# Batch 2's Q and K transposed by PE from 1 KB loads in an attention and MoE kernel, and x^T of batch 3 by DMA

## Chip, cores, metric

One core of one Trainium2 chip. The metric is device time in microseconds (us) of one execution. PE is TensorE (PEld its weight loads), DVE VectorE, ACT ScalarE, POOL GpSimd, and SP the queue that issues most DMAs. All of PE's matmuls in the profile write to the tiles o, acc, h and st; the program puts these in PSUM and calls them banks. All comparisons use fast runs (granted TensorE clock 0.99 to 1.00). A ratio is the mean time of one kernel's fast runs over that of the other's in the same rounds on the same chip, so it isn't quite the ratio of the medians quoted beside it.

## The reference, cut to what matters

```python
# q, k, v: (8 batches, 8 heads, 576 positions, 64)
scores = q @ k.T / 8;  keep 0 <= i - j < 64;  softmax;  attn @ v      # sliding window
x = attn_out.transpose(0, 2, 1, 3).reshape(4608, 512)
h = x @ w_in                                   # 512 x 2048
out = (h * clip(h + 3, 0, 6) / 6) @ w_out      # 2048 x 512
```

## The kernel before

The token axis is cut into nine tiles of 512. Tile T runs stage 1 (16 groups of 4 matmuls with w_in; ACT and DVE make the gate of each group) and stage 2 (64 matmuls with w_out). Attention of a later batch is threaded between the groups: `SS` (scores, exponent on ACT, mask product on DVE), `N_` (P times V and the normalization on DVE), and x^T either by PE (`X_`, 5 transposes and a copy on ACT) or by DMA (`xt_dma`). Heads go in pairs g = 0 to 3.

Q and K have to be transposed too. Batches 0 and 1 are loaded in 1 KB rows and transposed by PE, batches 2 to 7 are loaded in 256-byte rows, cast on POOL and transposed by DMA.

```python
def load_for_dma(b):                 # 256-byte rows, five loads each of q, k, v, on the SP queue
    ...
def transpose_pairs_by_dma(self):    # batch 2: eight DMA transposes
    for g in range(NG):
        for n, T in ((qn_all, self.QT), (kn_all, self.KT)):
            nc.sync.dma_start_transpose(out=T[:, g, :]..., in_=n[:, g, :, :, :]...)

def main_t(self, g, i, tr, copy=None):       # batches 0, 1: four PE transposes into PSUM tile tr
    ...
    def evac(): (copy or (vcopy, acopy)[i])(out=(self.QT, self.KT)[i]..., in_=tr...)  # Q by DVE, K by ACT
def rest_t(self, tr):                        # the last 64 positions of q and k, one PSUM tile
    ...
    def evac():
        vcopy(out=self.QT[:, :, SM:S], in_=tv[:, :, 0, :])
        (acopy if self.b else vcopy)(out=self.KT[:, :, SM:S], in_=tv[:, :, 1, :])

def s1_bank(fc, T):                          # PSUM of stage 1, group fc, here for T == 1
    if fc in (12, 13): ...                   # o, acc
    if fc % 4 < 2: return h_bank()[:]        # h0, h1
    return ...                               # st0, st1

def pieces(bt):                              # what follows group i of stage 1, piece i of stage 2
    if bt.b == 2:                            # in tile 1
        return p1, {1: [f(SS, 0)], 2: [f(SS, 1)], 4: [f(N_, 0), f(SS, 2)], 6: [f(X_, 0)], ...}
    if bt.b == 3:                            # in tile 2
        return {13: [f(SS, 0)]}, {0: [f(SS, 1)], 3: [f(N_, 0), f(SS, 2)], 5: [f(X_, 0)], ...}
    p1 = {10: [f(SS, 0)], 13: [f(SS, 1)]}    # batches 4 to 7: x^T by DMA
    p2 = {0: [f(SS, 2)], 1: [f(N_, 0)], 2: [f(SS, 3)], 3: [f(N_, 1), f(xt_dma, 0)], ...}
```

The softmax here doesn't subtract the row's maximum and nothing guards it: scores larger than these inputs give would overflow.

Of the kernel before, what the change touches and what calls it, by code (L numbers as in the profile page):

```python
# [24 lines left out]
def kernel(  # L25
# [9 lines left out]
    nc = tc.nc  # L35
    P = nc.NUM_PARTITIONS
# [3 lines left out]
    NG = H // 2  # L40
# [57 lines left out]
        return out  # L98

    class LoadsForPE:  # L100
        def __init__(self, b):
            self.b = b
            self.qst = stage.tile([P, H, R * D], F32, name="qst", tag="qst")
            self.kst = stage.tile([P, H, R * D], F32, name="kst", tag="kst")
            self.rst = stage.tile([P, H, D], F32, name="rst", tag="rst")
            self.tiles = (self.qst, self.kst, self.rst)

        def main(self, i, h0, h1):
            nc.gpsimd.dma_start(
                out=self.tiles[i][:, h0:h1, :],  # L110
                in_=(q, k)[i][self.b, h0:h1, 0:SM, :].rearrange("h (p j) d -> p h (j d)", j=R),
            )

        def rest(self):
            for i, src in enumerate((q, k)):
                nc.gpsimd.dma_start(
                    out=self.rst[i * SR : (i + 1) * SR, :, :],
                    in_=src[self.b, :, SM:S, :].rearrange("h s d -> s h d"),
                )

    def load_v_by_head(b):
        vst = stage.tile([P, KB, H, D], F32, name="vst", tag="vst")
        ins = load_blocks(vst, v, b, (KB - 1,), SR) + load_v(b, vst, 0, H)
        return vst, ins

    def load_for_dma(b):
        sts, ins = [], []
        for n, src in (("qst", q), ("kst", k), ("vst", v)):
            t = stage.tile([P, KB, H, D], F32, name=n, tag=n)
            ins += load_blocks(t, src, b, range(KB), SR if src is v else 0)  # L130
            sts.append(t)
        return tuple(sts), ins
# [34 lines left out]
    def keep_busy(n):  # L167
# [11 lines left out]
        out=mask1[:], in_=mask1[:], pattern=[[1, QW]], compare_op=ISGE,  # L179
# [3 lines left out]
        out=mask1[:], in_=mask1[:], pattern=[[-1, QW]], compare_op=ISGE,  # L183
        fill=0.0, base=WINDOW - 1, channel_multiplier=1,
    )
    qn_all = consts.tile([P, NG, KB, 2, D], BF16, name="qn")
    kn_all = consts.tile([P, NG, KB, 2, D], BF16, name="kn")
# [3 lines left out]
    for o0, m0, m1 in ((0, 0, QW), (QW, 0, QW), (2 * QW, 0, QW), (3 * QW, 0, P), (3 * QW + P, WINDOW, P)):  # L191
        nc.vector.tensor_scalar(
            out=maskneg[:, o0 : o0 + m1 - m0], in0=mask1[:, m0:m1],
# [45 lines left out]
    vcopy, pcopy, acopy = nc.vector.tensor_copy, nc.gpsimd.tensor_copy, nc.scalar.copy  # L239

    class Batch:
# [28 lines left out]
        def transpose_by_dma(self):  # L270
            for n, T in ((qn_all, self.QT), (kn_all, self.KT)):
# [1 line left out]
                    out=T[:].rearrange("d g (k s) -> d (g k) s", s=P),  # L273
                    in_=n[:].rearrange("p g k h d -> p (g k h d)"),
                )

        def transpose_pairs_by_dma(self):
            for g in range(NG):
                for n, T in ((qn_all, self.QT), (kn_all, self.KT)):
                    nc.sync.dma_start_transpose(  # L280
                        out=T[:, g, :].rearrange("d (k s) -> d k s", s=P),
                        in_=n[:, g, :, :, :].rearrange("p k h d -> p (k h d)"),
                    )

        def cast_qk(self, st, i, h0, heads, copy):
            n = (qn_all, kn_all)[i][:].rearrange("p g k h d -> p (g k h d)")[:, 0 : R * H * D]
# [237 lines left out]
    def s1(T, first=()):  # L524
        t0 = T * TB
        gT = gpool.tile([P, NFC, TB], BF16, name="gT")
        gTs[T] = gT

        def mms(fc, hT, gs):
            for g in gs:  # L530
                nc.tensor.matmul(  # L531
                    hT, lhsT=win16[:, g, fc * P : (fc + 1) * P],
                    rhs=xT[:, g, t0 : t0 + TB], start=(g == 0), stop=(g == NG - 1),
                )

        def gate(out, hT, shape):
            t1 = (t1pool, t2pool)[len(shape) - 2].tile(shape, BF16, name=f"t{len(shape) - 1}")
            nc.scalar.activation(out=t1[:], in_=hT, func=RELU, bias=half[:], scale=1.0 / 6.0)  # L538
            nc.vector.scalar_tensor_tensor(  # L539
                out=out, in0=t1[:], scalar=1.0, in1=hT, op0=MIN, op1=MULT,  # L540
            )

        if first:
            sts = [ps_st.tile([P, 2, 512], F32, name=f"st{u}") for u in range(2)]
            for gs in first:
                for fc in range(4):
                    mms(fc, sts[fc // 2][:, fc % 2, :], gs)
                yield
            for u in range(2):
                for fc in (2 * u, 2 * u + 1):  # L550
                    mms(fc, sts[u][:, fc % 2, :], (NG - 1,))
                gate(gT[:, 2 * u : 2 * u + 2, :], sts[u][:], [P, 2, TB])
                yield
                yield
        for fc in range(4 if first else 0, NFC):
            hT = s1_bank(fc, T)
            mms(fc, hT, range(NG))
            gate(gT[:, fc, :], hT, [P, TB])
            yield
# [25 lines left out]
    def run(gen, n=10 ** 6):  # L585
        for _ in range(n):
            if next(gen, "end") == "end":
                break
# [4 lines left out]
    def o_acc_tr():  # L593
        while True:
            yield ps_o.tile([P, 1024], BF16, name="o")
            yield ps_acc.tile([P, 1024], BF16, name="acc")

    oa_tr = o_acc_tr()
# [14 lines left out]
    def N_(bt, g, banks=None):  # L613
        n = [pv(bt, g, h, next(banks) if banks else h_bank()) for h in range(2)]
        n[0]()
        n[1]()

    def X_(bt, g, st=None):
        xt_pe(bt, g, h_tr() if st is None else ps_st.tile([P, 2, 1024], BF16, name=f"st{st}")[:, 0, :])()
# [17 lines left out]
    def cast_pairs(bt, st, h0, heads):  # L637
        bt.cast_qk(st, 0, h0, heads, pcopy)
        bt.cast_qk(st, 1, h0, heads, pcopy)


    bt, st = Batch(0), stage0
# [9 lines left out]
    ld = LoadsForPE(1)  # L652
# [9 lines left out]
    def T0_(g):  # L662
# [40 lines left out]
    m = s1(0, ((0, 1), (2,)))  # L703
# [12 lines left out]
        out=mask[:], in_=mask1[:].unsqueeze(1).to_broadcast([P, 2 * (KB - 1), QW])  # L716
    )
    for h in range(2):
        nc.vector.tensor_copy(
            out=mask[:, (KB - 1) * (h + 1) - 1, P:QW], in_=mask1[:, WINDOW : 2 * WINDOW],  # L720
        )
    bt, st = Batch(1), st1
# [18 lines left out]
    bt.cast_v_end(vst1, pcopy)  # L741
    for g in range(NG):
        bt.cast_v(vst1, 2 * g, 2 * g + 2, pcopy)
    st2, _ = load_for_dma(2)

    def st_tr(u):
        t = ps_st.tile([P, 2, 1024], BF16, name=f"st{u}")
# [2 lines left out]
    def st_pair(u):  # L750
        t = ps_st.tile([P, 2, 512], F32, name=f"st{u}")
        return iter((t[:, 0, :], t[:, 1, :]))
# [6 lines left out]
    m = s2(0, BY_PART)  # L759
# [33 lines left out]
    rest_x(bt0, 1)  # L793
    go()
    X_(bt, 0)
    N_(bt, 2, st_pair(0))
    X_(bt, 1, 1)
    N_(bt, 3, oa)
    X_(bt, 2)

    def stage_(T, bt, pieces1, pieces2):
        if T < 3:
            m = s1(T, ((0, 1), (2,)))
            run(m, 1)
            X_(Batch(T), NG - 1)
            run(m, 1)
        else:
            m = s1(T)
        for i in range(NFC):
            run(m, 1)  # L810
            for f in pieces1.get(i, ()):
                f()
        m = s2(T, BY_BLOCK)
        for i in range(16):
            run(m, 1)
            for f in pieces2.get(i, ()):
                f()

    def pieces(bt):
        if bt is None:  # L820
            return {}, {}
        f = lambda fn, *a: lambda: fn(bt, *a)
        p1, p2 = {}, {}
        if bt.b == 2:
            return p1, {
                1: [f(SS, 0)], 2: [f(SS, 1)], 4: [f(N_, 0), f(SS, 2)], 6: [f(X_, 0)], 7: [f(N_, 1), f(SS, 3)],
                9: [f(X_, 1)], 10: [f(N_, 2)], 12: [f(X_, 2)], 13: [f(N_, 3)],
            }
        if bt.b == 3:
            return {13: [f(SS, 0)]}, {  # L830
                0: [f(SS, 1)], 3: [f(N_, 0), f(SS, 2)], 5: [f(X_, 0)], 6: [f(N_, 1), f(SS, 3)],
                8: [f(X_, 1)], 9: [f(N_, 2)], 11: [f(X_, 2)], 12: [f(N_, 3)], 14: [f(X_, 3)],
            }
        p1 = {10: [f(SS, 0)], 13: [f(SS, 1)]}
        p2 = {
            0: [f(SS, 2)], 1: [f(N_, 0)], 2: [f(SS, 3)], 3: [f(N_, 1), f(xt_dma, 0)],
            5: [f(xt_dma, 1)], 6: [f(N_, 2)], 8: [f(N_, 3), f(xt_dma, 2)], 10: [f(xt_dma, 3)],
        }
        return p1, p2

    bt2 = Batch(2)
    bt2.cast_for_dma(st2, (0, 1))
    for u0, osb in held:
        nc.gpsimd.dma_start(out=out[u0 : u0 + P, :], in_=osb[:])
    bt2.cast_for_dma(st2, (2,))
    bt2.transpose_pairs_by_dma()
    nxt, pend = bt2, None
    for T in range(1, NTB):
        p1, p2 = pieces(nxt)
        b = T + 2  # L850
        nxt = None
        if b < B:
            sts, _ = load_for_dma(b)
            nxt = Batch(b)
            p1.setdefault(12 if T == 1 else 6, []).append(
                lambda bt=nxt, sts=sts: bt.cast_for_dma(sts)
            )
            p2.setdefault(6 if T < 3 else 12, []).append(lambda bt=nxt: bt.transpose_by_dma())
        stage_(T, None, p1, p2)


# [28 lines left out]
```

## Time and profile before

| | us |
|---|---|
| time, median of 4 fast runs | 313.4 (312.6 to 314.3) |
| profile that the prediction had | span 351.8, clock 0.85 (slow state) |
| profile taken later | span 314.8, clock 1.00 |

The first profile fell in the slow state. An experiment on another chip gave one at full clock. The stretches of it below are stage 1 and stage 2 of tile 1, then of tile 2. The columns are: stretch, its length, busy time and count of PE, PEld, DVE, ACT, POOL, clock, DMA share, GB/s.

```profile
58.94:73.78 14.84, 14.43 (x72) 6.52 (x70) 9.83 (x15) 10.71 (x15) 10.21 (x16) 1.00 1.04 211
73.78:94.06 20.28, 19.01 (x184) 10.45 (x183) 10.33 (x22) 10.32 (x16) 3.54 (x7) 1.00 0.96 187
94.06:109.74 15.68, 14.89 (x80) 6.80 (x79) 9.12 (x13) 11.68 (x17) 5.96 (x8) 1.00 1.03 227
109.74:128.25 18.51, 18.51 (x179) 10.42 (x178) 10.20 (x22) 9.53 (x15) 6.40 (x10) 1.00 1.13 211
```

A stage of pure matmuls (tiles 7 and 8) takes 13.81 us, 215.8 ns a matmul (12 of them take 2.59 us in the changed kernel's full-clock profile too, from 125.15 to 127.74). What is above that is attention's PE work or a wait.

### The profile page before, as it was taken

To read this page: it belongs to the slowest core of one execution; us is meant where nothing else is said; L and a number is where in the kernel's file an instruction comes from. 1 tells how busy PE (TensorE), PEld (TensorE's weight loads), DVE (VectorE), ACT (ScalarE), POOL (GpSimd) and SP (SyncE) were. 2 spreads that over 40 slices of the span, in tenths; PEclk is the share of its full clock that TensorE was granted. 3 is DMA by queue.
4 is the path that set the end of the run, shared out by engine and by line. 5 is a ranking of instruction groups with operands and counts; after the bars stand their busy time and mean duration, and the time that the engine had idled before them with its cause. 6 is when DMAs were issued, how large, how long until landed. Compare 5 with 4: busy or idle time off the path is not lost.

```text
span 351.8 us, 5579 instructions
## 1 busy us (share of the span) xinstructions
PE 339.5 (97%) x2125; PEld 158.6 (45%) x2162; DVE 177.9 (51%) x334; ACT 178.3 (51%) x264; POOL 94.1 (27%) x137
## 2 busy tenths in 40 slices
PE   7989998999999999999999999999999999999995
PEld 3534445444544554445444544454445444444442
DVE  4648546575418662776177616772477336106600
ACT  3757545566437644682268316831585146216511
POOL 6856355630540640334006500460000000000000
PEclk9888888888888888888888888888888888888888
DMA  7999999989999993992799669966600710010011
GB/s 250 174 255 234 210 170 215 211 208 185 195 212 251 208 231 110 218 181 69 193 221 213 122 162 235 197 136 128 168 3 30 113 53 0 31 61 30 0 61 60
DMA packets 147579, 52.80 MB, mean 150 GB/s; under 512 B 136384, under 2 KB 142528, under 8 KB 147552
## 3 DMA queue, kind: packets, MB, share of 16 engines
q1 hardware_dynamic: 141920, 44.18, 61.6%
q0 software_dynamic: 5360, 8.00, 11.4%
q8 instruction: 17, 0.28, 0.4%
q10 hardware_dynamic: 272, 0.26, 0.2%
q14 instruction: 10, 0.08, 0.1%
HBM read 36.70 MB, written 9.44 MB: 131 GB/s over the span
## 4 chain that ended last, share of the span: by engine, by line
PE 89%; DMA 4%; issue 2%; DVE 1%; ACT 1%; SPq 0%; POOL 0%; POOLq 0%
PE h L531 19%; PE o L568 19%; PE acc L568 18%; PE st L531 9%; PE o L531 7%; PE acc L531 7%; PE st L354 4%; DMA win<-in_moe_w_in_dram 2%; PE h L384 2%; PE h L568 2%; DMA qst<-in_q_dram 1%; PE h L389 1%; PE h L417 1%; ACT pT L362 1%; DMA vst<-in_v_dram 1%
## 5 line engine op out<-in xcount | busy, mean ns | idle before, releaser
L531 PEld LDWEIGHTS <-win 128*128 128x128 bf16 x576 | 59.6, 105 | 81.1 <-DMA win<-in_moe_w_in_dram 1.3
L568 PEld LDWEIGHTS <-gT 128*128 128x128 bf16 x576 | 56.3, 105 | 68.3 <-issue 0.5
L568 PE MATMUL o<-wout,gT 128*128 128x512 bf16 x261 | 73.0, 421 | 1.0 <-issue 0.3
L568 PE MATMUL acc<-wout,gT 128*128 128x512 bf16 x261 | 71.6, 421 | 0.8
L531 PE MATMUL h<-xT,win 128*128 128x512 bf16 x259 | 71.9, 421 | 0.4
L362 ACT ACTIVATE pT<-st 128x768 bf16<-128x768 f32 x64 | 48.8, 808 | 18.4 <-PE st L354 18.3
L539 DVE SCALAR_TENSOR_TENSOR gT<-t,st 128x512 bf16<-128x512 bf16 (+1 forms) x26 | 20.8, 809 | 69.5 <-ACT t L538 69.5
L538 ACT ACTIVATE t<-h,half 128x512 bf16<-128x512 f32 x66 | 44.7, 690 | 15.2 <-PE h L531 15.2
L539 DVE SCALAR_TENSOR_TENSOR gT<-t,h 128x512 bf16<-128x512 bf16 x66 | 44.6, 684 | 14.4 <-ACT t L538 14.4
L372 DVE TENSOR_TENSOR pT<-pT,mask 128x1536 bf16<-128x1536 bf16 x28 | 31.2, 1116 | 26.8 <-ACT pT L362 26.8
L258 POOL CAST qn<-qst 128x512 bf16<-128x512 f32 x24 | 14.8, 654 | 86.7 <-DMA qst<-in_q_dram 86.7
L531 PE MATMUL st<-xT,win 128*128 128x512 bf16 x124 | 34.3, 423 | 1.5 <-DMA win<-in_moe_w_in_dram 1.3
L574 ACT COPY osb<-acc 128x512 f32<-128x512 f32 x17 | 10.0, 586 | 49.8 <-PE acc L568 49.8
L574 ACT COPY osb<-o 128x512 f32<-128x512 f32 x17 | 10.0, 587 | 36.3 <-PE o L568 36.3
L531 PE MATMUL o<-xT,win 128*128 128x512 bf16 x91 | 26.9, 422 | 0.2
L531 PE MATMUL acc<-xT,win 128*128 128x512 bf16 x90 | 26.9, 422 | 0.2
L538 ACT ACTIVATE t<-st,half 128x512 bf16<-128x512 f32 (+1 forms) x26 | 20.1, 785 | 9.7 <-PE st L531 9.7
L406 DVE TENSOR_TENSOR opg<-h,rec 128x320 bf16<-128x320 f32 x48 | 23.6, 491 | 1.7
L384 PEld LDWEIGHTS <-pT 128*128 128x128 bf16 x256 | 18.6, 100 | 9.5 <-DVE opg L406 1.3
L248 POOL CAST V<-vst 128x512 bf16<-128x512 f32 (+1 forms) x14 | 17.3, 1233 | 18.5 <-DMA vst<-in_v_dram 15.9
L538 ACT ACTIVATE t<-acc,half 128x512 bf16<-128x512 f32 x23 | 15.8, 687 | 7.0 <-PE acc L531 7.0
L258 POOL CAST kn<-kst 128x512 bf16<-128x512 f32 x24 | 14.6, 648 | 17.4 <-DMA kst<-in_k_dram 14.4
(107 smaller groups left out, 293.4 us busy)
## 6 DMA issues: line engine op xcount, KB each, us to landing
out_dram<-osb SPq DMA_DIRECT2D x32, 256.0 KB, 2.3
qst<-in_q_dram SPq DMA_DIRECT2D x28, 256.0 KB, 4.6
kst<-in_k_dram SPq DMA_DIRECT2D x27, 256.0 KB, 5.3
vst<-in_v_dram SPq DMA_DIRECT2D x24, 256.0 KB, 5.4
vst<-in_v_dram SPq DMA_DIRECT2D x23, 128.0 KB, 4.6
win<-in_moe_w_in_dram POOLq DMA_DIRECT2D x4, 512.0 KB, 8.8
wout<-in_moe_w_out_dram POOLq DMA_DIRECT2D x4, 512.0 KB, 13.8
qst<-in_q_dram POOLq DMA_DIRECT2D x2, 512.0 KB, 12.3
```

The lines of the kernel that those rows point to most:

```text
L248: copy(out=self.V[:, 0 : KB - 1, h0:h1, 0:D], in_=vst[:, 0 : KB - 1, h0:h1, :])
L258: pcopy(out=n[:, g, 0 : KB - 1, :, :].rearrange("p k h d -> p k (h d)"), in_=s[:, 0 : KB - 1, 2 * g : 2 * g + 2, :].rearrange("p k h d -> ...
L354: nc.tensor.matmul(st[:, h, o0 : o0 + n], lhsT=bt.KT[h * D : (h + 1) * D, g, k0 : k0 + P], rhs=bt.QT[h * D : (h + 1) * D, g, q0 : q0 + n], ...
L362: nc.scalar.activation(out=pT[:, :, 2 * u : 2 * u + 2, 0:QW], in_=st[:, :, 0:w].rearrange("p h (k w) -> p h k w", k=2), func=EXP, scale=scale,
L372: nc.vector.tensor_tensor(out=pT[:, :, :, 0:QW], in0=pT[:, :, :, 0:QW], in1=mask[:].rearrange("p (h k) w -> p h k w", h=2), op=MULT,)
L384: nc.tensor.matmul(ob, lhsT=pT[:, h, qb, 0:P], rhs=V[:, qb, 2 * g + h, :], start=True, stop=(qb == 0),)
L406: nc.vector.tensor_tensor(out=opgs[bt.b, g][:, 0:nb, h, :], in0=ov[:, :, 0:D], in1=rec[:, 0:nb].unsqueeze(2).to_broadcast([P, nb, D]), op= ...
L531: nc.tensor.matmul(hT, lhsT=win16[:, g, fc * P : (fc + 1) * P], rhs=xT[:, g, t0 : t0 + TB], start=(g == 0), stop=(g == NG - 1),)
L538: nc.scalar.activation(out=t1[:], in_=hT, func=RELU, bias=half[:], scale=1.0 / 6.0)
L539: nc.vector.scalar_tensor_tensor(out=out, in0=t1[:], scalar=1.0, in1=hT, op0=MIN, op1=MULT,)
L568: nc.tensor.matmul(accs[ts], lhsT=gT[:, fc, ts * P : (ts + 1) * P], rhs=wout16[:, fc, :], start=(fc == 0), stop=(fc == NFC - 1),)
L574: acopy(out=osb[:], in_=accs[ts])
```

## The change

The intent is to relieve the DMA queues in the first third of the kernel, where they are full (a DMA share of 0.96 to 1.13 in the four stretches above): batch 2's q and k come in longer rows and need no DMA transposes, so that batch 3's loads start earlier. Batch 3 can then be treated like the later batches. PE pays with 36 transposes for batch 2 and saves 20 for x^T of batch 3.

```diff
-    st2, _ = load_for_dma(2)
+    ld = LoadsForPE(2, nc.sync)            # 512 KB loads in 1 KB rows, on SP
+    ld.main(0, 0, 4); ld.main(1, 0, 4); ld.rest(); ld.main(0, 4, 8); ld.main(1, 4, 8)
+    vst2, _ = load_v_by_head(2)
 ...                                        # end of stage 2 of tile 0
+    X_(bt, 1, 1)
     N_(bt, 2, st_pair(0))
-    X_(bt, 1, 1)
     N_(bt, 3, oa)
-    X_(bt, 2)                              # now, with X_(3), behind the first groups of tile 1
 ...                                        # pieces of batch 2, in tile 1
-            return p1, {1: [f(SS, 0)], 2: [f(SS, 1)], 4: [f(N_, 0), f(SS, 2)], ...}
+            t = lambda fn, *a: lambda: fn(bt, *a, oa_tr)      # PSUM tiles o and acc in turn
+            return {4: [t(TT, 0)], 6: [t(TT, 1)], 8: [t(TT, 2)], 9: [f(RR)], 10: [t(TT, 3)],
+                    13: [f(SS, 0)]},
+                   {0: [f(SS, 1)], 3: [f(N_, 0), f(SS, 2)], ...}
-        if bt.b == 3: ...                  # batch 3 takes the common places, with xt_dma
-    bt2.transpose_pairs_by_dma()
-            p2.setdefault(6 if T < 3 else 12, []).append(lambda bt=nxt: bt.transpose_by_dma())
+            p2.setdefault(6 if T < 2 else 12, []).append(lambda bt=nxt: bt.transpose_by_dma())
```

`TT(g)` is 8 PE transposes with a copy of Q^T by DVE and of K^T by ACT; `RR` is the same for the last 64 positions.

## The prediction

> **What bounds the kernel now.** I read the busy shares, the 40 slices, the table of stretches by stage, the waits of PE, and then the timeline of the DMA-issuing queue (SP) against that of PE.
>
> ```profile
> PE 339.5 (97%) x2125; PEld 158.6 (45%) x2162; DVE 177.9 (51%) x334; ACT 178.3 (51%) x264; POOL 94.1 (27%) x137
> ...
> PE   7989998999999999999999999999999999999995
> ...
> PEclk9888888888888888888888888888888888888888
> DMA  7999999989999993992799669966600710010011
> ```
>
> PE is busy 97% of the profiled span. But this execution is no timed one: its granted clock is 0.85 and its span 351.8 us (353.5 us for the run), whereas the timed runs take 313.6. The profile is in the slow state. So two things have to be read apart: what scales with the TensorE clock and what doesn't. DMA is full for the first 16 slices, some 140 us. In the slow profile that costs PE nothing; a faster PE may arrive before its data does.
>
> ```profile
> 19.40:61.90 42.50, 40.97 (x306) 20.48 (x311) 23.48 (x46) 23.94 (x36) 21.79 (x32) 0.85 1.12 218
> 61.90:80.60 18.70, 18.54 (x78) 7.79 (x77) 11.18 (x17) 11.42 (x16) 8.08 (x12) 0.85 0.96 202
> 80.60:114.40 33.80, 33.35 (x235) 16.66 (x240) 16.71 (x31) 18.97 (x27) 9.15 (x13) 0.85 1.08 215
> 114.40:137.90 23.50, 23.23 (x194) 12.52 (x198) 12.38 (x24) 11.88 (x18) 10.13 (x13) 0.85 1.06 192
> ```
>
> I cut at 19.4 (the first stage-1 matmul, released by the transfer of w_in), 61.9 (tile 1 begins), 80.6 and 114.4 (first scores of batches 2 and 3). The second number is PE busy: 59.5 of the 61.2 us from 19.4 to 80.6 and 33.35 of the next 33.8. The last two columns are the DMA share and GB/s.
>
> ```profile
> 50.02 5.99 SPq L94 DMA_DIRECT2D qst<-in_q_dram  x5
> 56.12 5.57 SPq L94 DMA_DIRECT2D kst<-in_k_dram  x5
> 61.80 6.40 SPq L94 DMA_DIRECT2D vst<-in_v_dram  x5
> 68.37 1.77 SPq L280 DMA_TRANSPOSE QT<-qn  x1
> 70.31 2.33 SPq L280 DMA_TRANSPOSE KT<-kn  x1
> ...
> 79.32 1.27 SPq L280 DMA_TRANSPOSE KT<-kn  x1
> 80.64 4.47 SPq L94 DMA_DIRECT2D qst<-in_q_dram  x5
> 85.15 6.63 SPq L94 DMA_DIRECT2D kst<-in_k_dram  x5
> 91.89 5.54 SPq L94 DMA_DIRECT2D vst<-in_v_dram  x5
> ...
> 98.20 4.50 SPq L272 DMA_TRANSPOSE QT<-qn  x1
> 102.80 2.75 SPq L272 DMA_TRANSPOSE KT<-kn  x1
> ```
>
> SP issues almost without a pause from 43.5 to 105.6 us: loads of batch 2 (18 us), its eight transposes (12.3 us), loads of batch 3, its two transposes. No step there waits for PE in substance[...]. By the landings, the first pair of batch 2 is in at 75.3 us (KT issued at 70.3, 5.0 us to landing) and batch 3 at 107.2 (KT issued at 102.8, 4.4 us).
>
> ```profile
> 80.61 0.53 PE L354 MATMUL st<-QT,KT 64*128 64x192 bf16 x10
> ```
>
> The scores of batch 2 begin at 80.6 us, 5.3 us after their data, those of batch 3 at 114.4, 7.2 us after theirs. In the slow profile that is slack.
>
> **Now at full clock**, which I assume for the timed runs: 59.5 x 0.85 = 50.6, with the 1.7 us idle 52.3, so PE reaches batch 2's scores at 71.7 us and stands for some 3.6 us until 75.3. From there 33.35 x 0.85 + 0.45 = 28.8 us to batch 3's: 104.1 us, against a landing at 107.2, another 3.1 us. The rest, 233.7 us to the end of PE and a tail of 3.7, becomes about 199 + 3.7. Sum: 107.2 + 202.7 = 310, and 1.7 us between span and run: 311.6, against 313.6 measured (312.6 the fastest). Without the two stalls, 6.7 us, it would be 305, too low. So the stalls are an inference that the total supports, not a wait seen in the profile.
>
> [...]
> - [...]one core, and 0.85 granted; 8 matmuls of 512 columns in 1.99 us, 249 ns each[...]
> [...]
> - [...]256-byte loads of 256 KB land 1.1 to 1.2 us apart (some 220 GB/s), and batch 1's 512 KB loads in 1 KB rows 1.5 us apart (36.4 and 37.9 us; 350 GB/s).
> [...]
>
> **The change, part by part.**
> - PE gains 32 transposes of q/k and 4 of the rest for batch 2. Eight take 0.49 us:
>
> ```profile
> 42.88 0.41 PE L317 MATMUL st<-ident,qn 128*128 128x128 bf16 x4
> 43.12 0.41 PE L317 MATMUL st<-ident,kn 128*128 128x128 bf16 x4
> 43.37 1.17 PE L568 MATMUL acc<-wout,gT 128*128 128x512 bf16 x4
> ```
>
>   4 x 0.49 + 0.28 = 2.2 us at 0.85, 1.9 at full clock. It loses the 20 transposes of batch 3's x^T (5 in 0.31 us): 4 x 0.31 = 1.24, or 1.05. Net +0.9 us on the path, as PE sets the end; [...]call it +1.2.
> - ACT and DVE gain the copies out of PSUM in stage 1 of tile 1: DVE 4 x 0.69 + 0.28 = 3.0, ACT 4 x 0.58 + 0.37 = 2.7 us, and the first scores of batch 2 as well (1.6 us ACT, 1.1 DVE). That stretch holds about 10 and 11 us of them in 16.6 us; at full clock about 14 and 15 in some 16: tight, but still beside PE. I allow 0.3 us.
> - DMA: nine q/k loads (11.5 us) become four of 512 KB in 1 KB rows (4 x 1.5) and two small ones (2 x 0.6): 7.2 us. So q/k of batch 2 are in by about 61 us instead of 65, cast by about 62.5. PE at full clock begins tile 1 at about 56 and wants the first transpose at 61 (its half cast by 58.5), the third pair at 65. No stall should be left, with 2.5 us to spare.
> - The eight DMA transposes (12.3 us of SP) go, so batch 3's loads follow batch 2's V at about 63 us instead of 80.6: batch 3's K^T lands at about 90, wanted at about 101 (its scores move to the common place, three matmul groups earlier). The second stall goes too.
> - Order at the end of stage 2 of tile 0: PE waits there 0.6 us for the normalized output of batch 1. Pair 2's transpose is moved behind the first matmuls, but these then need the bank that the same normalization reads. The wait moves; I count no gain.
> - x^T of batch 3 by DMA: for batch 4 the last lands at 170.9 and tile 4 starts at 174.2. The same pattern a tile earlier: free.
>
> Sum: 313.6 - (4 to 6.7, centre 5.6) + 1.2 = 309.2.
>
> **Rivals.**
> - *The timed clock is about 0.96 and PE never waits.* For it: 351.8 x 0.85/0.96 is about 312, and the profile shows no DMA wait on PE beyond the one at 19.4. Against it: some partial throttle would have to repeat within 0.5% in three runs. Then only +1.2 us is left: 314 to 315.
> - *The stalls are larger, or DMA moves slower beside a faster PE.* Every microsecond by which batch 2 and 3 come late is won back: 305 to 307. Against it: the total leaves no room for much over 7 us.
> - *The wait is replaced.* ACT or DVE becomes the bound in stage 1 of tile 1, or batch 2's casts on POOL come late behind V of batch 1 (done at 55.2). Then 1 to 3 us of the gain go: 310 to 312.
>
> **Range and chances.** Full clock with stalls of 4 to 7 us, about 75%: 307.5 to 311. No stall, about 15%: 314 to 315. A larger gain about 10%. Faster by 2% means below 307.4, at the near edge of the main case: 0.25. Slower by 2% (above 319.9) needs a new wait of 6 us that nothing shows: 0.04. Range 306 to 313.5.
>
> **What would show it.** A changed profile at clock 0.85 should be no faster, some 352 to 353 us, with tile 1's stage 1 about 2.5 to 3 us longer and stages 2 of tiles 1 and 2 shorter. A changed profile at full clock should show no wait of PE on QT or KT, batch 3's loads issued at about 63 us, and its K^T in by about 90. Each transpose group costing 0.4 us would confirm the PE term. The prediction is wrong if the kernel before, profiled at full clock, shows no PE wait at the scores of batches 2 and 3, or if ACT or DVE releases PE throughout tile 1's stage 1.

## The result, and the profile after

317.6 us is the median of the three fast runs, which took 316.5 to 318.1 (a fourth, profiled one took 449.0 at a clock of 0.66 and is left out; with it the median is 317.9). The ratio is 1.0127 (95% interval 1.0079 to 1.0175): slower by 4 us. On another chip, in five rounds, it was 1.0129 (1.0101 to 1.0156). There the output passed the comparison with the reference. That says little: two runs below whose scores of batch 2 are wrong passed it too.

The profile of that first job is slower still than the one before, at a granted clock of 0.66:

```profile
PE 434.7 (97%) x2140; PEld 185.0 (41%) x2178; DVE 179.4 (40%) x339; ACT 179.6 (40%) x265; POOL 93.3 (21%) x138
...
PEclk8666666666666666666666666666666666666666
```

At 0.66 PE waits only 0.4 us in all on the copies of Q^T, which at full clock will turn out to be the main loss, so I read the changed kernel from a second one at full clock (span 317.9 us). These are the same four stages:

```profile
59.24:79.45 20.21, 17.44 (x120) 9.08 (x121) 12.54 (x20) 13.52 (x22) 11.81 (x21) 1.00 1.25 247
79.45:97.69 18.24, 18.24 (x175) 10.15 (x174) 10.35 (x22) 9.18 (x15) 7.34 (x8) 1.00 0.96 193
97.69:113.36 15.67, 15.37 (x91) 7.09 (x90) 9.56 (x13) 12.34 (x19) 4.26 (x8) 1.00 1.14 194
113.36:131.19 17.83, 17.19 (x149) 8.75 (x148) 10.42 (x21) 5.84 (x10) 5.87 (x6) 1.00 0.74 139
```

Stage 1 of tile 1 grew by 5.4 us, from 14.84 to 20.21, though PE is busy there for only 17.44. Stage 2 gave back 2.0, as the first scores left it and a K^T wait is gone. Tile 2 gave back 0.7. All later stages are equal within 0.2 us.

I use sums over these four stages and stage 1 of tile 3 (14.90 us) below, because the time before tile 1 differs between profiles: it began at 57.2 to 61.3 us, mostly with the landing of w_in (see "Placement in memory"). The sum is 86.8 for the changed kernel, and 84.2, 83.5 and 83.2 in three profiles that have the kernel before's work in them (itself, the one with the order alone, the one with an idle tile), 83.6 on average. **The difference is 3.2 of the 4.0 us.**

Where PE stands in stage 1 of tile 1, from its timeline; the bracket is the idle time before an instruction and what ended it:

```profile
64.14 0.39 PE L309 MATMUL o<-ident,qn 128*128 128x128 bf16 x4
...
67.80 0.38 PE L309 MATMUL o<-ident,qn 128*128 128x128 bf16 x4 [1.31 <-DVE QT L314]
...
75.46 1.02 PE L523 MATMUL o<-xT,win 128*128 128x512 bf16 x4 [1.27 <-DVE QT L314]
```

PE wants PSUM tile o for the next pair, and then for matmul group 12, while the Q^T before is still in it. DVE and ACT at the same time:

```profile
64.19 2.35 DVE L531 SCALAR_TENSOR_TENSOR gT<-t,st 128x1024 bf16<-128x1024 bf16 x2 [3.84 <-ACT t L530]
66.46 0.68 DVE L531 SCALAR_TENSOR_TENSOR gT<-t,h 128x512 bf16<-128x512 bf16 x1
67.06 0.68 DVE L314 COPY QT<-o 128x512 bf16<-128x512 bf16 x1
...
74.11 0.69 DVE L531 SCALAR_TENSOR_TENSOR gT<-t,st 128x512 bf16<-128x512 bf16 x1 [1.03 <-ACT t L530]
74.72 0.68 DVE L314 COPY QT<-o 128x512 bf16<-128x512 bf16 x1
```

```profile
73.12 0.37 ACT L300 COPY KT<-h 128x256 bf16<-128x256 bf16 x1 [0.96 <-DVE QT L299]
```

The first Q^T, in PSUM at about 64.5, is copied at 67.06: in DVE's timeline the two double-size gates of the stage's opening groups (2.35 us from 64.19 on) and one more gate (0.68 us) come first. PE wants the tile from 66.49 on; 0.57 us of its wait lie before the copy begins and 0.68 in the copy. The last one, in PSUM at about 73.1, is copied at 74.72 (PE wants the tile from 74.19 on, so 0.53 and 0.68 us): DVE stands idle for 1.03 us before a gate, waiting for ACT, and ACT had stood idle for 0.96 us, waiting for DVE to finish its copy from the PSUM tile that ACT's own copy reads too. DVE is busy 12.5 and ACT 13.5 of these 20.2 us: neither is full.

### The profile page after: what moved, and what is told of

Its sections match the earlier page's. It is cut to its first block, busy times and chain, and to the rows that moved or that the text cites. A ratio compares the mean times of both kernels' runs of the same rounds, so it can differ in the third digit from the quotient of the medians.

```text
span 447.3 us, 5619 instructions
## 1 busy us (share of the span) xinstructions
PE 434.7 (97%) x2140; PEld 185.0 (41%) x2178; DVE 179.4 (40%) x339; ACT 179.6 (40%) x265; POOL 93.3 (21%) x138
## 4 chain that ended last, share of the span: by engine, by line
PE 95%; issue 1%; DVE 1%; DMA 1%; ACT 1%; POOL 0%
PE o L560 20%; PE acc L560 19%; PE h L523 19%; PE st L523 9%; PE acc L523 7%; PE o L523 7%; PE st L346 4%; PE h L560 2%; PE h L376 2%; PE h L381 1%; PE h L409 1%; PE st L334 1%; DMA qst<-in_q_dram 1%; PE h L309 1%; PE h L387 0%
## 5 line engine op out<-in xcount | busy, mean ns | idle before, releaser
L523 PEld LDWEIGHTS <-win 128*128 128x128 bf16 x576 | 68.0, 121 | 109.9 <-issue 106.7
L560 PEld LDWEIGHTS <-gT 128*128 128x128 bf16 x576 | 64.8, 119 | 97.3 <-issue 92.9
L560 PE MATMUL o<-wout,gT 128*128 128x512 bf16 x263 | 93.5, 509 | 1.3 <-issue 0.4
L560 PE MATMUL acc<-wout,gT 128*128 128x512 bf16 x260 | 90.8, 512 | 1.5 <-issue 0.4
L523 PE MATMUL h<-xT,win 128*128 128x512 bf16 x256 | 91.2, 512 | 1.0 <-issue 0.4
L523 PE MATMUL st<-xT,win 128*128 128x512 bf16 x125 | 44.7, 511 | 1.3 <-DVE rec L395 0.9
L523 PE MATMUL acc<-xT,win 128*128 128x512 bf16 x91 | 34.3, 512 | 0.1
L523 PE MATMUL o<-xT,win 128*128 128x512 bf16 x90 | 33.6, 513 | 0.7 <-DVE QT L314 0.4
L395 DVE RECIPROCAL rec<-h 128x5 f32<-128x5 f32 x48 | 9.0, 187 | 34.2 <-PE h L387 34.2
L346 PEld LDWEIGHTS <-KT 64*128 64x128 bf16 x312 | 12.0, 100 | 23.4 <-issue 20.0
```

The lines of the kernel that those rows point to most:

```text
L346: nc.tensor.matmul(st[:, h, o0 : o0 + n], lhsT=bt.KT[h * D : (h + 1) * D, g, k0 : k0 + P], rhs=bt.QT[h * D : (h + 1) * D, g, q0 : q0 + n], ...
L395: nc.vector.reciprocal(out=rec[:, 0:nb].unsqueeze(2), in_=ov[:, :, D:VW])
L523: nc.tensor.matmul(hT, lhsT=win16[:, g, fc * P : (fc + 1) * P], rhs=xT[:, g, t0 : t0 + TB], start=(g == 0), stop=(g == NG - 1),)
L560: nc.tensor.matmul(accs[ts], lhsT=gT[:, fc, ts * P : (ts + 1) * P], rhs=wout16[:, fc, :], start=(fc == 0), stop=(fc == NFC - 1),)
```

## The experiments

Eighteen runs were made: the kernel before once more (a single look), the changed kernel once more, and sixteen other kernels, all but the look in five rounds beside the kernel before. The number in parentheses after a ratio is its 95% interval.

### The kernel before, once more

No edit.

> The kernel before again, for a profile at full clock. Theory of the prediction (DMA stalls at full clock): PE idle 3 to 3.6 us before the first scores of batch 2 and about 3 us before those of batch 3. Rival (PE never waits for DMA): no such idle time, PE idle in all under 4 us after the first 20 us.

This gave the full-clock profile above, clock 0.998. The scores of batches 2 and 3 do wait for K^T, but for much less than predicted:

```profile
76.74 0.51 PE L354 MATMUL st<-QT,KT 64*128 64x192 bf16 x10 [1.07 <-DMA KT<-kn]
...
107.56 0.51 PE L354 MATMUL st<-QT,KT 64*128 64x192 bf16 x10 [0.49 <-DMA KT<-kn]
```

It is 1.6 us together (0.6 and 0.7 in two other profiles of the same work). There was little to win.

### The two halves of the change, and its order alone

```diff
# e1: the changed kernel, batch 3 as before
+        if bt.b == 3: return {13: [f(SS, 0)]}, {0: [f(SS, 1)], 3: [f(N_, 0), f(SS, 2)], 5: [f(X_, 0)], ...}
-    6 if T < 2 else 12
+    6 if T < 3 else 12
# e2: the kernel before, batch 3 like the later ones
-        if bt.b == 3: ...
-    6 if T < 3 else 12
+    6 if T < 2 else 12
# e3: the kernel before with the change's order at the end of tile 0 and the start of tile 1
```

> The batch-2 part alone (1 KB loads, transposes by PE, new order at the end of tile 0), batch 3 keeps x^T by PE. The change as a whole measured +4.2 us (313.4 to 317.6). Theory A (the work that PE, ACT and DVE gained in stage 1 of tile 1 is the loss, no stall was there to win): 317 to 319, slower than before by 4 to 5 us, as the 20 transposes of batch 3 come back (+1.1). Theory B (x^T of batch 3 by DMA is late or its scores are badly placed): 312 to 314.5. The prediction's own sum would have it at 310.

> The batch-3 part alone (x^T by DMA, scores in the common places, batch 4's transposes at piece 12), batch 2 as before. Theory A: 312 to 313, some 1 us faster as 20 PE transposes go. Theory B: 316 to 318. If K^T of batch 3 lands late at full clock, as the prediction had it, scores three groups earlier wait longer and the time rises by up to 2.5 us: then 314 to 316.

> Only the order at the end of stage 2 of tile 0 and the start of tile 1 (the transposes of pairs 2 and 3 of batch 1 behind the first matmuls of tile 1). Theory A says 313.2 to 314 (the wait moves from the transpose to the bank). Rival C (the order costs: PE waits for the bank st0 and for x^T): 314.5 to 316.

- Batch-2 part: 318.8 us, 1.0109 (1.0065 to 1.0153). Stage 1 of tile 1 takes 20.21 us as in the whole change, with the same two waits (1.31 and 1.27).
- Batch-3 part: 319.4 us, 1.0135 (1.0094 to 1.0176). Its loss is mostly in tile 2, where the scores of batch 3 now come three groups earlier while their K^T comes hardly earlier (in at 105.73 us); another 0.8 us is in stage 1 of tile 3, where PE waits 0.6 us for x^T. Its PE timeline in tile 2:

```profile
105.78 0.51 PE L354 MATMUL st<-QT,KT 64*128 64x192 bf16 x10 [3.03 <-DMA KT<-kn]
106.22 1.48 PE L531 MATMUL h<-xT,win 128*128 128x512 bf16 x4
```

 What comes after the idle time is slow too: four matmuls take 1.48 us instead of 1.03, at a granted clock of 0.59 from 106.3 to 108.5 us (1.00 from 102.5 to 105.7).
- Order alone: 315.2 us, 1.0003 (0.9973 to 1.0032).

Neither half is good alone, each for its own reason: the second needs the first to get its K^T in time. In the whole change no PE wait on K^T is left.

### PE's transposes alone

```diff
# f2: the kernel before, in tile 1 after groups 4, 6, 8, 9, 10
+    nc.tensor.transpose(out=tr[...], in_=win16[:, j % NG, 0:P], identity=ident[:])   # x 36, results unread
```

> The kernel before with 36 transposes more in stage 1 of tile 1, at the places of the change, of a constant that is in SBUF anyway, their results unread (the output is right). It measures the PE term alone: the prediction had 1.9 us (8 in 0.49 us at 0.85 clock). Theory A2: +1.9 to 2.2 us, 1.006 to 1.007 of before. Rival (transposes between other matmuls cost more than their time in a row): +3 us and more.

315.2 us, 1.0015 (0.9997 to 1.0034): +0.5 us. The stretch of stage 1:

```profile
57.49:73.64 16.15, 16.15 (x109) 8.55 (x107) 9.84 (x15) 10.80 (x15) 10.40 (x17) 1.00 1.14 230
```

PE is busy for all of it. The transposes take 2.0 us (0.45 us a pair in the changed kernel, four times, and 0.22), but stage 1 is only 1.3 us longer, and stage 2 with 19.15 us 1.1 shorter than in the look at the kernel before, since K^T has landed meanwhile. (In the profile with the idle tile stage 2 took 19.15 us too: there K^T was in time without more transposes, so how much is absorbed differs between executions.) Part of this work of PE falls where it would have waited. So PE's own time alone isn't the loss.

### The changed kernel again

> The changed kernel again, for a profile at full clock. Theory A2 (from the batch-2 part alone: 20.2 us in stage 1 of tile 1, of which two waits of 1.3 us on the DVE copies of Q^T): the same stretch of about 20 us with the same two waits; tile 2 then 15.1 + 16.9 us, 1.7 us shorter than before; in all 1.005 to 1.015 of before. Rival (the batch-3 part brings a wait of its own, x^T by DMA late at the start of tile 3 as in the batch-3 part alone): PE waits 0.5 us or more on x^T at tile 3.

319.0 us, 1.0129 (1.0101 to 1.0156). Its lines are shown above. Both waits are there. Tile 3 starts without a wait on x^T (14.90 us in stage 1), against the rival. But stage 2 of tile 2 takes 17.83 us, where the same stage takes 16.87 in the batch-3 part alone. From the timelines of POOL, DVE and PE there:

```profile
118.66 1.90 POOL L248 CAST V<-vst 128x2048 bf16<-128x2048 f32 x1 [3.16 <-PE o L560]
```

```profile
119.00 2.36 DVE L364 TENSOR_TENSOR pT<-pT,mask 128x1536 bf16<-128x1536 bf16 x1 [0.55 <-ACT pT L354]
```

```profile
122.05 0.23 PE L376 MATMUL h<-V,pT 128*128 128x65 bf16 x2 [0.42 <-DVE opg L398]
```

DVE's mask product takes 0.96 us when no POOL cast runs beside it (11 of 28 here). Here it ends 0.8 us after a 1.9 us cast that began before it.

### POOL's cast of V in four pieces

```diff
# h1
-                self.cast_v(st[2], 0, H, pcopy)
+                for h in range(0, H, 2):
+                    self.cast_v(st[2], h, h + 2, pcopy)
```

> The changed kernel with POOL's cast of V (one instruction of 1.9 us) cut into four of some 0.6 us, batches 3 to 7. In the changed kernel the mask product on DVE that met this cast took 2.36 us instead of 0.96, and stage 2 of tile 2 took 17.84 us instead of 16.87. Theory D (DVE waits out the POOL instruction): no mask product over 1.7 us, stage 2 of tile 2 17.0 to 17.4, ratio about 0.002 below the changed kernel's. Rival (chance, or a different cause): no change.

317.5 us, 1.0078 (1.0041 to 1.0114). No mask product over 1.38 us, and stage 2 of tile 2 down from 17.83 to 16.95. The same product now:

```profile
117.99 0.96 DVE L365 TENSOR_TENSOR pT<-pT,mask 128x1536 bf16<-128x1536 bf16 x1 [0.35 <-ACT pT L355]
```

In this profile the meeting didn't happen: V landed later, and the first quarter of the cast began at 119.23, after the product. The three profiles below in which a quarter of the split cast does meet this product (both edits; later places with split casts; the spread version) show what the split does: 1.37, 1.36 and 1.02 us instead of 2.36. Stage 2 of tile 2 took 16.85 to 17.01 us in all four profiles with split casts. In the variants of the whole change with the whole cast it took 17.8 to 18.2 in the five where the two met (one of them the faulty run of the later places), and 16.88 and 17.17 in two where they happened to miss each other.

In all twenty profiles of this case together, each of the 38 mask products that begins inside a cast of V and takes over 0.96 us ends 0.80 to 0.81 us after that cast. What holds the product back until then wasn't shown. So in the changed kernel's profile 0.9 us of batch 3's gain was lost to a collision that the new timing brought.

### More banks, and both

```diff
# g2: pairs 1 and 3 into the halves of st1; the groups of stage 1 use h0, h1, st0 in turn
-                4: [t(TT, 0)], 6: [t(TT, 1)], 8: [t(TT, 2)], 9: [f(RR)], 10: [t(TT, 3)],
+                4: [t(TT, 0)], 6: [lambda: TT(bt, 1, st_tr(1))], 8: [t(TT, 2)], 9: [f(RR)],
+                10: [lambda: TT(bt, 3, st_tr(1))],
# gh: g2 and h1
```

> The changed kernel, same transposes at the same places, but pairs 1 and 3 go to the two halves of bank pair st1 (the matmul groups of that stage then use h0, h1 and st0 in turn). No transpose and no matmul group has to wait for the DVE copy before it in its own bank. Theory A3 (half of the loss is PE waiting for a bank until DVE, in order behind its gates, has copied Q^T out): both waits of 1.3 us go, stage 1 of tile 1 takes 17.5 to 18 us instead of 20.2, ratio to before 1.003 to 1.007. Rival (DVE and ACT are simply full there, the wait moves to the next bank): 19.5 to 20.2 us, ratio 1.011 to 1.014.

> Both edits. If the two add: 3 to 3.5 us less than the changed kernel, ratio to before 1.000 to 1.005.

More banks: 318.1 us, 1.0092 (1.0060 to 1.0125). Both waits on o go, but stage 1 of tile 1 falls only from 20.21 to 19.52, as the rival had it. The waits of PE in it:

```profile
PE h L291 <- DVE gT L535: 0.8, 1, 0.8
PE h L527 <- DVE gT L535: 0.4, 2, 0.2
```

They moved to the matmul groups' own banks, of which there was one less. With both edits: 316.9 us, 1.0065 (1.0048 to 1.0082), short of the 1.000 to 1.005 expected.

### A quarter of the copies

```diff
# c1: Q^T and K^T of batch 2 wrong on purpose
-    in_=tr[:, 0:SM].rearrange("d (j p) -> d p j", p=P)
+    in_=tr[:, 0:SM].rearrange("d (j p) -> d p j", p=P)[:, 0 : (32 if self.b == 2 else P), :]   # out too
```

> The changed kernel with each copy of Q^T and K^T of batch 2 out of PSUM cut to a quarter of its columns: the scores of batch 2 are then wrong on purpose. PE does the same work in the same order. Theory A4 (the loss in stage 1 of tile 1 is the time of the copies on DVE and ACT, which are full there, so that it comes back to PE by whichever bank it needs next): stage 1 of tile 1 takes 17 to 17.6 us instead of 20.2, the two waits of 1.3 us mostly go, ratio to before 1.002 to 1.006. Rival (the banks or the places of the transposes alone): over 19 us.

317.3 us, 1.0115 (1.0075 to 1.0154). A copy takes 0.28 us instead of 0.68, and each of the two waits shrinks by just that:

```profile
PE o L309 <- DVE QT L314: 0.9, 1, 0.9
PE o L523 <- DVE QT L314: 0.9, 1, 0.9
```

Stage 1 is 19.41 us. **So the theory that DVE and ACT are full with copies fell:** what goes from each wait is the 0.4 us by which its own copy is shorter, and the part before the copy begins stays (0.56 us before the first copy here, 0.57 in the changed kernel). The comparison with the reference passed here too, though the scores of batch 2 are wrong.

### Later places

```diff
# f1: pairs 0 to 2 after groups 5, 7, 9, pair 3 in stage 2
-  {4: [t(TT, 0)], 6: [t(TT, 1)], 8: [t(TT, 2)], 9: [f(RR)], 10: [t(TT, 3)], 13: ...}, {0: [f(SS, 1)], 3: ...}
+  {5: [t(TT, 0)], 7: [t(TT, 1)], 9: [t(TT, 2)], 10: [f(RR)], 13: ...}, {0: [f(SS, 1)], 1: [f(TT, 3)], 3: ...}
# f3: f1, and the casts of batch 3 after that TT(3)
# f4: f3 and h1
```

> The changed kernel with the transposes of batch 2 after groups 5, 7 and 9 instead of 4, 6, 8, 10, the last pair moved into stage 2. Theory A2 (the bank waits on the DVE copy that is queued behind the backlog of double-size gates are over half of the loss): both waits under 0.5 us, stage 1 of tile 1 near 17 to 17.5 us, the whole 2 to 2.6 us less than the changed kernel, 1.002 to 1.006 of before. Rival (the PE time of the transposes is the loss): no faster than the changed kernel by over 0.5 us.

> The run with the later transposes, mended: there the casts of batch 3 overwrote batch 2's K before its last pair was transposed; they now come after it. Theory A4: stage 1 of tile 1 near 18.2 us as there, stage 2 18.3 to 18.8, no wait on POOL: 1.3 to 1.9 us less than the changed kernel, ratio to before 1.007 to 1.010, provided that K^T of batch 3 still lands in time. If it lands late, a K^T wait in stage 1 of tile 2 takes the gain back.

> The same with POOL's V casts split. If the two add: stage 2 of tile 2 at 17.0 us as well, ratio to before 1.003 to 1.007, the best of the changed kernels; no version is expected to beat the kernel before.

The first of these was my mistake: the casts of batch 3 into the shared buffer stood ahead of the last transposes of batch 2 in the program. PE waited 3.2 us for them and transposed the wrong batch's K; the comparison with the reference let it pass. Its time, 323.2 us, says nothing about the places. Mended: 317.2 us, 1.0105 (1.0065 to 1.0145), stage 1 of tile 1 18.23 us and stage 2 18.94, so 1.3 us less for the two together, with one wait of 0.8 us left. The timed gain is 0.5 to 1 us; the intervals overlap. With the split casts: 316.3 us, 1.0062 (1.0041 to 1.0083).

### One copy moved, and the spread version

```diff
# r1: the copy of the rest's K^T
-    (acopy if self.b else vcopy)(out=self.KT[:, :, SM:S], ...)
+    (acopy if self.b == 1 else vcopy)(out=self.KT[:, :, SM:S], ...)
# r2: f4 and r1, pairs 0, 1 after groups 5, 8, pairs 2, 3 in stage 2
```

> The changed kernel with one copy moved: K^T of the rest of batch 2 goes out of PSUM by DVE, right after Q^T, instead of by ACT, which stood idle 0.96 us for DVE's copy out of the same bank. Theory A5 (no engine is full in stage 1 of tile 1, but ACT, DVE and PE work in order and wait for each other in turn; the second wait of 1.3 us hangs on that ACT idle time): the ACT wait goes, the second wait on bank o falls from 1.3 to 0.5 us or less, stage 1 of tile 1 19.2 to 19.6 us. The first wait stays at 1.3. Rival (DVE's added work is what counts): unchanged or longer.

> The mended run with split casts, the rest copies on DVE, pair 1 three groups after pair 0, pairs 2 and 3 in stage 2 of tile 1. Theory A5: no wait over 0.4 us on a copy of Q^T; stage 1 of tile 1 16.2 to 16.8 us, stage 2 18.9 to 19.5, tile 2 as with split casts (32.6): 35.5 + 32.6 against 35.0 + 33.6 before, so 0.995 to 1.001 of before. If K^T of batch 3 comes too late, tile 2 shows a wait and the ratio is over 1.003.

With the one copy moved, ACT's idle time on DVE's copy goes, and the second wait follows, though not as far as expected (ACT now stands idle 0.74 us there for a gate of DVE's):

```profile
PE o L309 <- DVE QT L314: 1.3, 1, 1.3
...
PE o L523 <- DVE QT L314: 0.8, 1, 0.8
```

The first wait is untouched, as expected; stage 1 is 19.72 us (19.2 to 19.6 expected). The ratio of 1.0077 (1.0048 to 1.0106) is lower than the changed kernel's by 0.5%; this profile was itself a slow run, so I rest on the wait.

The spread version missed its forecast: it has 16.88 us in stage 1 and 20.04 in stage 2 of tile 1 (16.2 to 16.8 and 18.9 to 19.5 expected), where one wait of 0.8 us on a copy of Q^T is left, now on a bank h. Over the five stages it has 84.3 us, 0.7 more than the kernel before. It is timed at 317.1 us, 1.0063 (1.0040 to 1.0085), which is 2.0 us. **No version beat the kernel before.**

### x^T of batch 3 by DMA, scores left late

```diff
# v1: the kernel before; batch 3 keeps SS after group 13, xt_dma after pieces 4, 7, 10, 12
-   5: [f(X_, 0)], ... 14: [f(X_, 3)]
+   4: [f(xt_dma, 0)], 7: [f(xt_dma, 1)], 10: [..., f(xt_dma, 2)], 12: [f(xt_dma, 3)]
# also: N_ up to two pieces earlier, batch 4's transposes after piece 14, tile 3 begun with three pairs
```

> The kernel before with x^T of batch 3 by DMA, but with the scores of batch 3 left where they were (after group 13), and tile 3 begun with the three pairs that land first. The batch-3 part alone lost 4.2 us. Theory E (that loss is K^T of batch 3 landing after the moved scores want it, not the DMA for x^T): no K^T wait over 0.7 us, PE work 20 transposes less: 1 to 1.5 us faster than before, ratio 0.995 to 0.998. Rival (x^T by DMA comes late): PE waits on x^T at the start of tile 3, ratio 1.002 or more.

319.5 us, 1.0144 (1.0099 to 1.0188). The K^T wait in tile 2 falls to 0.7 us, but then x^T comes late:

```profile
PE st L531 <- DMA xT<-opg: 3.2, 2, 2.3
```

Its first transpose is issued only at 124.2 us. So both halves of my theory E and of its rival are seen: with batch 2 still transposed by DMA, batch 3 by DMA is late, at K^T or at x^T.

### Placement in memory

```diff
# z1: the kernel before with one tile of 1 KB a partition more
# z2: the changed kernel sharing that tile between batches
```

> The kernel before with the one tile of 1 KB a partition more that the changed kernel allocates, and one memset on it. In the profiles the changed kernels enter tile 1 about 1 us later on average than those like the kernel before (58.9 against 57.6 us), mostly because the first part of w_in lands later, which no line of the change touches. If the placement of tiles in memory does it: ratio 1.002 to 1.005. If it is chance: 0.998 to 1.002.

> The changed kernel with that tile shared between batches 1 and 2, so that its memory is laid out as before. If the placement does it: about 1 us less than the changed kernel, ratio 1.009. If it is chance: 1.011 to 1.014.

0.9998 (0.9979 to 1.0017) and 1.0105 (1.0066 to 1.0143). The first excludes the 1.002 to 1.005 of the theory; the second fits both theories. So the placement isn't it, as far as the first shows. The later start of tile 1 in some profiles goes with w_in's landing; in three of them that wait (2.3, 1.6 and 1.6 us) was followed by a lower granted clock (0.50 from 22 to 25 us with the one copy moved, 0.51 from 19.5 to 22.9 us with more banks, 0.8 in the third slice of the spread version's page). Whether chance alone makes it isn't settled.

## Why the prediction was wrong, step by step

It said 309.2 with 306.0 to 313.5; measured were 317.6 (317.9 with the slow run in the median). Two steps failed: the stalls that were to be won (step 2) and the copies that were to cost 0.3 us (step 5).

1. **Full clock in the timed runs: right** (0.997 to 0.999). The rival with 0.96 and no stall was wrong in its clock.
2. **"59.5 x 0.85 = 50.6, with the 1.7 us idle 52.3, so PE reaches batch 2's scores at 71.7 us and stands for some 3.6 us": wrong, the term mis-sized first.** PE reached them at 75.67 (76.74 less the wait of 1.07) and K^T was ready at 76.7. Two things failed. A busy PE at a reduced clock wasn't time that scales here: stage 2 of tile 0 took 24.9 us at 0.85 and still 23.2 to 24.4 in five full-clock profiles with the same work there, instead of 21.2. And a matmul takes 215.8 ns at full clock, where 249 x 0.85 is 212. The 4 us at the low end of the stalls and the centre of 5.6 (the sum gave 6.7) were the author's estimates. That SP's line would keep its slow-profile times at full clock was an estimate too: K^T of the first pair was in at 76.7 us at full clock, at 75.3 in the slow profile. The second stall was 0.49 instead of 3.1. Together they were worth 0.6 to 1.6 us instead of 5.6, the largest error.
3. **"So the stalls are an inference that the total supports": wrong.** The sum of 311.6 came near 313.6 with too little PE time and too much stall. A total can't confirm its parts.
4. **Cost of the PE transposes: right.** 1.9 predicted, 2.0 measured, and only 0.5 us of time when they are added alone. The 0.3 us from the net +0.9 to the +1.2 of the sum were the author's estimate.
5. **"tight, but still beside PE. I allow 0.3 us": wrong, and the largest loss.** It measured 2.6 us (1.31 and 1.27), and the sum (-5.6 + 1.2) doesn't even have the 0.3: its 1.2 is PE's term alone. The third rival, "The wait is replaced", named this stage and these engines with 1 to 3 us, but as a part of a gain that wasn't there. Busy shares were the wrong view: DVE and ACT are 62 and 67% busy. The copies stand in order behind gates, and one engine's wait becomes the next one's. Moving one copy took 0.5 us off one wait, quartering them 0.4 off each, other places 1.3 off the tile; no edit removed the loss, so its cause is shown in part. The chain of in-order waits is read from the timelines, and the edits agree with it; how much of the first wait is the double-size gates alone wasn't tested apart.
6. **DMA part: right in mechanism.** Batch 2's q and k were in at 62.3 us (predicted 61), batch 3's loads were issued from 65.8 (predicted 63), its K^T landed at 93.6 (predicted 90), and no K^T wait is left. The relief worked, but there was little to relieve (step 2).
7. **Order at the end of tile 0, no gain: right** (1.0003).
8. **x^T of batch 3 free, 1.05 us of PE saved: half right.** It came in time. But in the profile 0.9 us went into the collision of DVE's mask product with POOL's cast, which the prediction didn't look for.

Sum for the stages: +2.0 (transposes), +2.6 (two waits), about -1.0 (K^T waits) and -0.2 (tile 2 beyond its K^T waits) make 3.4, against 3.2 by the stages. The timed 4.0 (2.5 to 5.5) holds that; some 0.8 us are not placed. They may lie before tile 1, which the profiles with the new batch-2 part enter at 58.9 us on average and the others at 57.7; why is open.

## What to carry to other kernels

A wait inferred from scaling a slow profile is worth a look at a full-clock profile before work is moved for it: stage 2 of tile 0 hardly scaled here, and a total that fits proves no term. When work is added to PE, ask for the latency of what has to empty its PSUM tile: count the instructions ahead of that copy in its engine's order, not the engine's busy share (here 1.31 us of wait for 0.68 us of copy, with DVE 62% busy). And two changes that each lose alone can need one another; test the halves and the whole.

## What the traces showed of the hardware

- This one-core program was granted a clock of 0.85 and 0.66 in two profiled executions (351.8 and 447.3 us) and 0.99 to 1.00 in the others. What lowered it, and what else ran on those chips, isn't known.
- Idle times of 3.03 us (batch-3 part: 0.59 mean clock in the 2.2 us from 106.3 us on) and even 1.6 us (more banks: 0.51 from 19.5 to 22.9 us) were followed by a lower granted clock.
- One PE transpose of q or k lasted 219 to 246 ns in the slow profile, but in a row they came every 61 ns there, and eight in a row took 0.45 us at full clock.
- The last DMA transposes of batch 2, 164 KB each, landed 1.31 us apart in the slow profile (79.14, 80.45 and 81.77 us). That isn't the rate of the transfer: from 77 to 81 us the DMA engines moved up to 300 GB/s in bursts, with nothing in between. Each of the last six of the eight held SP for 1.21 to 1.27 us, and the next was issued right after, which is the pace seen.
- The release of a PSUM tile, behind other work in the copying engine's order, cost more than the copy: 0.68 us of copy, 1.3 us of PE wait.
